# Changing the order in which a wide block's second half sums its chunks, and the way of the first decay rows, in a kernel of decay attention and a softplus feed-forward

## The chip, the cores and the metric

The kernel runs on one core of a Trainium2 chip. The core has five engines that run side by side, each through its own list of instructions, strictly in the order in which they were written out: TensorE (PE, matrix products), VectorE (DVE), ScalarE (ACT), GpSimd (POOL) and SyncE (SP), which here only issues DMA transfers. ACT can issue transfers too. An engine that waits for one instruction holds up all that stand behind it in its list. The metric is the device time of one execution in microseconds (us).

## The reference

Eight batches of eight heads, 576 positions, 64 values per head; then a feed-forward over 4608 tokens of 512 values, with 2048 hidden ones.

```python
scores = scale * np.matmul(q, k.transpose(0, 1, 3, 2))
cum = np.cumsum(np.log(np.clip(f, 0.0001, 1.0)), axis=-1)
decay = cum[:, :, :, None] - cum[:, :, None, :]
scores = np.where(causal, -1000000000.0, scores + decay)
attn = softmax(scores)                      # over the last axis
x = np.matmul(attn, v)                      # heads joined: 4608 x 512
h = x @ w_in                                # 512 x 2048, given as float64
g = np.maximum(h, 0.0) + np.log1p(np.exp(-np.abs(h)))
return g @ w_out                            # 2048 x 512, given as float64
```

## The kernel before, in words

**An order planned on the host.** The kernel does not write instructions straight out. It collects operations (`add`), each with the engines that may do it, a cost in us (`on_pe`, `on_act`, `on_dve`, `on_dma`, ...), what it comes after, and which buffers it takes (`takes`) and gives back (`give`). `Plan.run` (L93 on) then simulates the engines with these costs: among the next 700 operations it picks the one that can start earliest by its own clock, writes it out on its engine, and goes on. So the costs decide the order on every engine; the chip then keeps that order, whatever the real durations are. A DMA's cost on SP is `max(0.6 n, kb / 360)` for n transfers and kb kilobytes, and `dma_lag` adds the time until the data has landed. Where the plan foresees a gap of PE above 0.5 us at the start, it writes dummy matmuls into it (L1320), and `WARM` more at the very start (L1309), to keep PE's clock up.

**The start.** `decay` (L358) loads f for all 64 heads (64 partitions x 576), clips it (L366), takes the logarithm (L369), sums it along the row in one scan (L374, tile `cum`) and stores the sums to DRAM (`cum_d`, L377). The split of the sums into a rounded part and a rest (L382, L383) and its store for later heads (`aug_d`, L387) follow when the second early job has been set up. The sums enter the scores as two further rows (64 and 65) of the tile `T` that holds a head's q and k: `rows` reads them from `cum_d` (L639 for a pair of half heads, L644 and L645 for a whole one).

**Attention.** The heads of batch 0 are worked first in single pass float32: four jobs of two half heads each (256 positions), then eight with the rest. Then come 56 heads with every operand split in two (rounded to PE's fast format, and the rest). A job makes scores (L747, or L749 and L750), subtracts the row maximum (L754, DVE), takes exponents into `p` (L774, ACT), scales by the row sums (L796, L798), transposes (L831) and multiplies by v (L880, L886). The tiles `p` are set to zero once at the start (`ps_set`), and every exponent waits for all of these fills.

**Weights.** The float64 weights come in 32 pieces of 512 KB (L432), each turned into float32 by one ACT and four DVE operations (L436 to L451; L439 on POOL or DVE). All loads of weights, and the q and k of the third and later jobs, wait for `first_rows`: the landing of the first decay rows. All these loads share SP's queue.

**The feed-forward** runs over blocks of tokens as their attention ends: two blocks of 256 tokens (the first in plain float32, L1024 and L1147), then eight wide ones of 512. For a wide block PE makes 16 chunks of the hidden layer (L1043, 12 matmuls a chunk; `up_part`), each of which goes through the gate (L1076 to L1098) into two tiles `gh` and `gl`, three buffers each. The sums with w_out (L1128, three matmuls per chunk and tile of 128 tokens) need a PSUM bank per tile for the whole sum over 16 chunks, and only two banks `acc` are there. So in six of the eight wide blocks the first two tiles are summed while the gates come (`down_part`), `finish` copies both banks out and stores them (L1215), and the other two tiles are summed afterwards (`second`): the half of each chunk that they need has been stored to `g_d` after the gate (L1102) and is loaded back in pairs of chunks (L1179) into the same `gh` and `gl` buffers. The two last wide blocks have four banks and no second half. Sums of one block are chained in the order in which they are added. Up to six units at the end of a second half are mixed with the next block's first chunks; attention is mixed in throughout.

Of the kernel before, what the change touches and what calls it, by code (L numbers as in the profile page):

```python
# [10 lines left out]
F32 = mybir.dt.float32  # L11
# [12 lines left out]
WINDOW = 700  # L24
PLAIN = 0
WARM = 7
# [149 lines left out]
def on_dma(kb, n=1, eng="SP"):  # L176

    return On(eng, max(0.6 * n, kb / 360 if eng == "SP" else 0.0))


def dma_lag(kb, n=1, eng="SP"):
    return 0.6 * (n - 1) + 2.1 + kb / n / 360 - on_dma(kb, n, eng).cost
# [30 lines left out]
def tile_decay_attention_softplus_ffn(  # L213
# [87 lines left out]
    cum_d = dpool.tile([BH, S], F32, name="cum_d")  # L301
# [54 lines left out]
    decay_ready, cum_used, first_rows = {}, [], []  # L356

    def decay():  # L358
# [12 lines left out]
        def scan(e):  # L371

            box["c"] = buf("x32", [P, NCC, S], "cum")[0:BH, 0, :]
            e.tensor_tensor_scan(box["c"], box["f"], box["f"], 0.0, ALU.add, ALU.min)  # L374

        def store_first(e):
            e.dma_start(out=cum_d, in_=box["c"])  # L377

        def split(e):
            hl = buf("raw", [P, 2, S], "chl", F32R)  # L380
            ch, cl = box["hl"] = hl[0:BH, 0, :], hl[0:BH, 1, :]
            e.tensor_copy(ch, box["c"])  # L382
            e.tensor_sub(cl, box["c"], ch.bitcast(F32))  # L383
# [8 lines left out]
        c = add(On("DVE", 1.36), scan, after=[l], takes=("x32",))  # L392
        give("wl", [c])
        decay_ready["sums"] = add_dma(store_first, BH * S / 256, after=[c])
        cum_used.append(add(NO_ENGINE, mark, after=[decay_ready["sums"]]))
        def rest():
            s = add(On("DVE", 1.05, 0.0, True), split, after=[c], takes=("raw",))
# [178 lines left out]
    def attention(job):  # L576
# [28 lines left out]
        def load_v():  # L605
# [14 lines left out]
            st["v"] = add_dma(v, 128 if pair else 160, takes=(vtag,))  # L620
            st["V"] = [st["v"]]

        def load32():
# [8 lines left out]

            def rows(e):
                if pair:

                    t0 = T0[number // 2 % 2].rearrange("p t s -> p (t s)")[:, 0:2048]
                    t0 = t0.rearrange("p (i t s) -> p i t s", i=4, t=2)
                    for x in range(2):
                        e.dma_start(  # L639
                            out=t0[64 + x : 65 + x, :, x],  # L640
                            in_=cum_d[bh : bh + 4, 0:256].unsqueeze(0),
                        )
                else:
                    e.dma_start(out=qk32[64:65, 0, qs:qe], in_=cum_d[bh : bh + 1, qs:qe])  # L644
                    e.dma_start(out=qk32[65:66, 1, 0:ke], in_=cum_d[bh : bh + 1, 0:ke])  # L645
# [6 lines left out]
            if not pair:  # L652
                y = add_dma(rows, 4, 2, after=[start, decay_ready["sums"]] + set_)
            elif number % 2:
                y = rows_of[number - 1]
            else:
                need = [start, decay_ready["sums"]] + set_ + T0_set[number % 4 + 1, 1]
                y = rows_of[number] = add_dma(rows, 8, 2, after=need)
                first_rows[:] = first_rows or [y]
            st["T"] = [x, y]  # L660
# [66 lines left out]
        def stat_tile(ti):  # L727
# [42 lines left out]
            for a, z, acc, box in todo:  # L770
# [5 lines left out]
                x = add(on_act(z - a, 0.19, True), weight, after=mins + [st["p"]] + ps_set)  # L776
# [183 lines left out]
    def ffn_block(i):  # L960
# [109 lines left out]
        def gate(u):  # L1070
# [46 lines left out]
            if ahead < ntile:  # L1117
# [5 lines left out]
        def products(e, fc, tiles, gh, gl):  # L1123

            for n, tt in enumerate(tiles):
                lh, ll = (x[:, n * P : (n + 1) * P] for x in (gh, gl))
                for m, (l, r) in enumerate(((lh, woh), (lh, wol), (ll, woh))):
                    e.matmul(  # L1128
                        st["acc", tt], l, r[fc],
                        start=fc == 0 and m == 0, stop=fc == NFC - 1 and m == 2,  # L1130
# [6 lines left out]
        def down_part(u, k):  # L1137
            box, ready, kept = st["g", u]
            fc = u * nk + k
            tags = (("acc", "acc") + late_banks)[:ahead]  # L1140

            def mm(e):
                if fc == 0:
                    begin(range(ahead), tags)
# [7 lines left out]
                products(e, fc, range(ahead), *(box[x][:, k * nt :] for x in "hl"))  # L1152

            op = add(
                on_pe32(DM * ahead) if plain else on_pe(DM, 3 * ahead), mm,
# [7 lines left out]
            if k == nk - 1:  # L1163
# [248 lines left out]
```

## Time and profile before

| | |
|---|---|
| median of 3 runs | 1227.53 us (1227.13 to 1228.07) |
| the profiled execution | 1227.12 us |
| its span, first to last instruction | 1225.1 us |
| PE, DVE, ACT, POOL busy | 1199.9, 869.5, 872.9, 137.4 us |
| mean granted clock of PE | 0.999 |
| moved by DMA | 168.38 MB, mean 137 GB/s |

The profile is of one execution. A busy time is the time in which at least one instruction of the engine was under way. Matmuls overlap, so a single one lasts longer (0.39 us for 512 columns) than the distance to the next. The chain of work that ended last is followed back from the last instruction, at each step to what released it. In the timeline, what stands in brackets behind an instruction is the time its engine stood idle before it and what ended that.

### The profile page before, as it was taken

The numbers are of one execution on the slowest core, as the hardware profiler recorded it, in microseconds if no ns is written. First come the engines' busy times: TensorE is split into PE (matmuls) and PEld (weight loads), VectorE is DVE, ScalarE is ACT, GpSimd is POOL, SyncE is SP. The second block draws the span as 40 slices with busy tenths as digits, with TensorE's granted clock in tenths as the row PEclk, the third lists the DMA queues.
The fourth block names the chain that finished last, engine by engine and source line by source line (L and its number), as shares of the span: only waits on it lengthen the run. The fifth ranks groups of instructions, "written<-read, shape, count | busy, mean of one in ns | idle before, by whom it ended". The sixth has DMA issues, their size and how long they took to land.

```text
span 1225.1 us, 19553 instructions
## 1 busy us (share of the span) xinstructions
PE 1199.9 (98%) x6320; PEld 993.9 (81%) x6320; DVE 869.5 (71%) x2164; ACT 872.9 (71%) x2120; POOL 137.4 (11%) x128
## 2 busy tenths in 40 slices
PE   7899999999999999999999999999999999999998
PEld 5666678888887888888888888888888888888886
DVE  6998889998787678877787778677866774223322
ACT  4676688878787788778886788788867873444543
POOL 3632012010001000110010100110010000000000
PEclk9999999999999999999999999999999999999999
DMA  7874435435446543744464446453565425211210
GB/s 199 254 207 143 137 91 153 111 90 166 128 141 179 166 133 117 228 145 128 137 197 136 141 130 197 139 168 104 153 186 155 138 80 172 69 52 52 86 52 35
DMA packets 100198, 168.38 MB, mean 137 GB/s; under 512 B 10496, under 2 KB 74008, under 8 KB 100096
## 3 DMA queue, kind: packets, MB, share of 16 engines
q1 hardware_dynamic: 100096, 167.13, 46.2%
q8 instruction: 50, 0.82, 0.3%
q14 instruction: 52, 0.43, 0.1%
HBM read 127.85 MB, written 39.24 MB: 136 GB/s over the span
## 4 chain that ended last, share of the span: by engine, by line
PE 84%; DVE 6%; DMA 4%; ACT 4%; issue 1%; SPq 1%; POOL 1%; DVEq 0%; POOLq 0%; ACTq 0%
PE h L1043 29%; PE acc L1128 28%; PE b L831 7%; PE o L886 6%; PE s L750 3%; PE s L749 3%; PE h L1024 2%; PE acc L1147 2%; PE o L880 2%; DMA raw<-in_qkT 2%; PE s L747 1%; ACT p L774 1%; DVE s L754 1%; DMA xh_st<-in_w_in 1%; DVE pl L846 1%
## 5 line engine op out<-in xcount | busy, mean ns | idle before, releaser
L1043 PE MATMUL h<-xh,wih 128*128 128x512 f32 (+1 forms) x576 | 229.5, 401 | 0.7 <-DVE pl L846 0.3
L774 ACT ACTIVATE p<-s,negm 128x288 f32<-128x288 f32 (+7 forms) x384 | 183.0, 479 | 50.3 <-DVE negm L754 46.6
L1043 PE MATMUL h<-xl,wih 128*128 128x512 f32 (+1 forms) x576 | 216.7, 379 | 0.0
L1090 DVE SCALAR_TENSOR_TENSOR h<-h,e 128x512 f32<-128x512 f32 x136 | 95.2, 700 | 136.0 <-ACT e L1082 135.9
L754 DVE CUSTOM_DVE_ANT_0 s<-s,cmask 128x288 f32<-128x288 f32 (+5 forms) x320 | 137.8, 436 | 72.1 <-PE s L750 61.6
L798 POOL TENSOR_SCALAR p<-p,rsum 128x448 f32<-128x448 f32 (+4 forms) x79 | 89.4, 1139 | 784.5 <-PE s L750 192.6
L1076 ACT ACTIVATE e<-h 128x512 f32<-128x512 f32 x144 | 85.7, 595 | 126.4 <-PE h L1043 124.5
L846 DVE TENSOR_TENSOR pl<-b,ph 128x64 fp32r<-128x64 f32 (+1 forms) x224 | 126.3, 569 | 35.0 <-ACT ph L209 33.1
L1043 PE MATMUL h<-xh,wl 128*128 128x512 f32 (+1 forms) x576 | 148.7, 380 | 0.0
L1128 PE MATMUL acc<-woh_dt_float32r,gh 128*128 128x512 f32 x352 | 143.1, 406 | 0.0
L1128 PE MATMUL acc<-woh_dt_float32r,gl 128*128 128x512 f32 x352 | 138.0, 392 | 0.0
L1128 PE MATMUL acc<-wol_dt_float32r,gh 128*128 128x512 f32 x352 | 137.3, 390 | 0.0
L831 PE MATMUL b<-ident,p 128*128 128x128 f32 x784 | 126.5, 274 | 4.8 <-POOL p L798 2.6
L1043 PEld LDWEIGHTS h<-xh,wih 128*128 128x128 f32 x576 | 108.8, 189 | 17.1 <-DVE gl L1098 0.8
L1043 PEld LDWEIGHTS h<-xh,wl 128*128 128x128 f32 x576 | 104.8, 188 | 21.7
L1043 PEld LDWEIGHTS h<-xl,wih 128*128 128x128 f32 x576 | 108.8, 189 | 14.6
L1098 DVE TENSOR_TENSOR gl<-h,gh 128x512 fp32r<-128x512 f32 x136 | 93.4, 687 | 35.1 <-ACT gh L209 34.1
L209 ACT CAST ph<-b 128x512 fp32r<-128x512 f32 (+1 forms) x171 | 85.3, 501 | 41.7 <-PE b L831 40.4
L831 PEld LDWEIGHTS b<-ident,p 128*128 128x128 f32 x784 | 94.4, 140 | 22.6 <-ACT p L796 3.5
L796 ACT ACTIVATE p<-p,rsum 128x192 f32<-128x192 f32 (+6 forms) x219 | 108.6, 556 | 3.4 <-DVE rsum L787 2.8
L749 PE MATMUL s<-T 128*64 128x64 f32 x336 | 98.2, 304 | 2.0 <-ACT p L774 1.3
L886 PE MATMUL o<-ph,vhl 128*128 128x448 f32 (+4 forms) x352 | 98.6, 294 | 0.0
(159 smaller groups left out, 2402.2 us busy)
## 6 DMA issues: line engine op xcount, KB each, us to landing
wl<-wil_d SPq DMA_DIRECT2D x72, 512.0 KB
raw<-in_qkT SPq DMA_DIRECT2D x112, 288.0 KB
g_d<-gh SPq DMA_DIRECT2D x96, 128.0 KB
g_d<-gl SPq DMA_DIRECT2D x96, 128.0 KB
vr<-in_vR SPq DMA_DIRECT2D x64, 160.0 KB
out<-ob SPq DMA_DIRECT2D x36, 256.0 KB
sto<-in_w_out SPq DMA_DIRECT2D x11, 512.0 KB
sti<-in_w_in SPq DMA_DIRECT2D x9, 512.0 KB
```

What stands on the lines that cost most here:

```text
L749: e.matmul(o, qA[:, q0:end], kA[:, a:z], start=True, stop=False)
L754: e.tensor_tensor_reduce(out=box["o"], in0=box["o"], in1=cmask[0:n_q, right - w : right], scale=-0.125, scalar=m0 if i else 3.0e38, op0=AL ...
L774: e.activation(o, box["o"], AF.Exp, bias=m1, scale=-1.0, accum_out=acc)
L796: e.activation(a, a, AF.Copy, scale=f_)
L798: e.tensor_scalar(a, a, f_, None, ALU.mult)
L831: e.transpose(box["ps"][:, at : at + P], pt[pi][:, c : c + P], one)
L846: e.tensor_sub(box["l"], box["ps"][:, 0:w], box["h"].bitcast(F32))
L886: e.matmul(box["ps"][:, a - g0 : z - g0], st["vhl"][:, vc, :], pbox[x][:, o : o + z - a], start=i == 0 and m == 0, stop=i == len(todo) - 1 ...
L1043: e.matmul(o, l, r, start=m == 0, stop=m == 11)
L1090: e.scalar_tensor_tensor(h, h, 0.0, box["e"], ALU.max, ALU.add)
L1098: e.tensor_sub(box["l"], box["t"], box["h"].bitcast(F32))
L1128: e.matmul(st["acc", tt], l, r[fc], start=fc == 0 and m == 0, stop=fc == NFC - 1 and m == 2,)
```

## The change

Three things are changed together.

First, the start. The scan is cut in two, columns 0 to 255 and the rest. The decay rows are no longer stored to DRAM and read back: they are copied from the tile of the sums into the rows of `T`. For a pair of half heads each of the two rows is one transfer of its own, on SP for the first pair of jobs and on ACT's queue for the second. `first_rows`, for which the loads of weights wait, is now the first part of the scan. The fills of `p` wait for the first part of the scan, the ones used first stand first, and an exponent waits only for the fill of its own tile. The split of the sums and its store come in the third round of jobs, after an output of the first. `WARM` falls from 7 to 3.

Second, the plan's model of a transfer: 262 GB/s (`kb / 262` us) instead of 360, and 1.5 us of the engine for one on another queue than SP's.

Third, the change from the first to the second half of a wide block. Chunks 14 and 15 are not stored to `g_d` and not loaded back; their gate tiles are kept. Their sums run tile by tile: tile 0 with chunks 14 and 15, its copy, tile 1 with both, its copy, then tiles 2 and 3 with both, out of the kept gate tiles, as the first addends of their banks; then chunks 0 to 13 as before.

```diff
+RATE = 262
-WARM = 7
+WARM = 3
 def on_dma(kb, n=1, eng="SP"):
-    return On(eng, max(0.6 * n, kb / 360 if eng == "SP" else 0.0))
+    return On(eng, max(0.6 * n, kb / RATE) if eng == "SP" else 1.5 * n)
 def dma_lag(kb, n=1, eng="SP"):
-    return 0.6 * (n - 1) + 2.1 + kb / n / 360 - on_dma(kb, n, eng).cost
+    each = 0.6 if eng == "SP" else 1.5
+    return each * (n - 1) + 2.1 + kb / n / RATE - on_dma(kb, n, eng).cost
...
-            e.tensor_tensor_scan(box["c"], box["f"], box["f"], 0.0, ALU.add, ALU.min)
-        def store_first(e):
-            e.dma_start(out=cum_d, in_=box["c"])
+            c = cum[0] = buf("x32", [P, NCC, S], "cum")[0:BH, 0, :]
+            x = box["f"][:, 0:256]
+            e.tensor_tensor_scan(c[:, 0:256], x, x, 0.0, ALU.add, ALU.min)
+        def scan_rest(e):
+            c = cum[0]
+            x = box["f"][:, 256:S]
+            e.tensor_tensor_scan(c[:, 256:S], x, x, c[:, 255:256], ALU.add, ALU.min)
...
+            later = first_rows if 3 < number < nplain else []
+            st["v"] = add_dma(v, 128 if pair else 160, after=later, takes=(vtag,))
...
+            def rows2(e, x):
+                e.dma_start(out=t0[64 + x : 65 + x, :, x], in_=cum[0][bh : bh + 4, 0:256])
...
-                y = rows_of[number] = add_dma(rows, 8, 2, after=need)
-                first_rows[:] = first_rows or [y]
+                y = rows_of[number] = [
+                    add_dma(lambda e, r=r: rows2(e, r), 4, eng="ACT" if number else "SP", after=need)
+                    for r in range(2)
+                ]
+                first_rows[:] = [decay_ready["first"]]
...
-                x = add(on_act(z - a, 0.19, True), weight, after=mins + [st["p"]] + ps_set)
+                x = add(on_act(z - a, 0.19, True), weight, after=mins + [st["p"], ps_set[number % 2, pi]])
...
-            if ahead < ntile:
+            if ahead < ntile and u < NFC - 2:
                 d = add_dma(keep, 256, 2, after=[h_, l_] + kept_read.get(u, []))
...
         def second(fp, k, tiles=range(ahead, ntile)):
             fc = 2 * fp + k
+            first, here = fc == NFC - 2, fp == NFP - 1
             def mm(e):
+                if first:
+                    begin(tiles, ("acc",) * 2)
+                o = (tiles[0] - ahead) * P
+                if here:
+                    g = (st["g", fc][0][x][:, TB + o :] for x in "hl")
+                else:
+                    g = (st[x, fp][:, k * TB + o :] for x in ("gh", "gl"))
+                products(e, fc, tiles, *g, first, fc == NFC - 3)
...
+            downs[-2:] = [[], []]
+            for tt in range(ahead):
+                downs[-1] += [
+                    (down_t / 2, lambda u=u, tt=tt: down_part(u, 0, [tt]))
+                    for u in (NFC - 2, NFC - 1)
+                ] + [(0.0, lambda tt=tt: finish([tt]))]
+            for tt in range(ahead, ntile):
+                tail += [
+                    (down_t / 2, lambda k=k, tt=tt: second(NFP - 1, k, [tt])) for k in range(2)
+                ]
+            tail += [
+                (down_t, lambda fp=fp, k=k: second(fp, k)) for fp in range(NFP - 1) for k in range(2)
             ] + [(0.0, lambda: finish(range(ahead, ntile)))]
...
-        if n == 1:
-            decay_rest()
...
+        if n == 2:
+            decay_rest(wrote[0][0][2:])
```

94 lines of the change are left out of this document (43 added, 51 removed).

## The prediction

> **What bounds the kernel now.** I read the page first: its busy totals, then the same in stretches, then the chain that ended last, then the single waits of PE.
>
> ```profile
> PE 1199.9 (98%) x6320; PEld 993.9 (81%) x6320; DVE 869.5 (71%) x2164; ACT 872.9 (71%) x2120; POOL 137.4 (11%) x128
> ```
>
> PE is busy for 98% of the span, so a change that leaves the matrix work as it is can only win what PE does not use. Part of the 98% is no work, though. The groups by line have 29.6 us of fill, matmuls that compute nothing, and the timeline (start, us, engine, line, operation) has 6.5 us of warming; the other rows of the timeline are used further down:
>
> ```profile
> L1320 PE MATMUL fill<-cmask 128*128 128x128 f32 x210 | 29.6, 293 | 2.4 <-POOL cmask L307 2.4
> ```
>
> ```profile
> 4.54 1.86 POOL L307 MEMSET p<- 128x128 f32 x5
> ...
> 5.07 6.50 PE L1309 MATMUL warm<-cmask 128*128 128x448 f32 x14
> ...
> 7.50 2.04 DVE L307 MEMSET p<- 128x256 f32 x5
> ...
> 67.29 1.03 PE L1024 MATMUL h<-x,woh_dt_float 128*128 128x256 f32 x4
> ```
>
> Together 36.1 us, all before the first matmul of the feed-forward at 67.29. The busy time by stretches (PE, PEld, DVE, ACT, POOL; then granted clock, DMA share, GB/s) shows what the start waits for:
>
> ```profile
> 5.00:10.00 5.00, 5.00 (x13) 2.51 (x12) 4.29 (x8) 0.01 (x1) 1.40 (x4) 1.00 0.88 194
> 10.00:15.00 5.00, 5.00 (x36) 4.21 (x35) 0.15 (x1) 0.00 (x0) 0.00 (x0) 1.00 0.27 52
> 15.00:20.00 5.00, 4.12 (x24) 3.01 (x22) 4.57 (x23) 4.47 (x18) 2.45 (x4) 1.00 0.95 256
> 20.00:25.00 5.00, 3.17 (x18) 2.23 (x19) 2.55 (x8) 2.04 (x6) 0.00 (x0) 1.00 1.04 237
> ...
> 25.00:50.00 25.00, 19.61 (x127) 16.02 (x126) 22.53 (x50) 16.77 (x40) 14.11 (x10) 0.93 0.80 264
> 50.00:75.00 25.00, 23.27 (x138) 17.93 (x138) 24.66 (x61) 17.79 (x43) 12.85 (x6) 1.00 0.84 235
> ...
> 75.00:175.00 100.00, 100.00 (x460) 66.30 (x460) 87.61 (x224) 72.15 (x178) 16.20 (x12) 1.00 0.49 141
> 75.00:1200.00 1125.00, 1116.36 (x5871) 928.60 (x5871) 802.08 (x1998) 821.03 (x1998) 102.37 (x88) 1.00 0.45 134
> ```
>
> Between 10 and 15 us nothing works: DVE 0.15 us, ACT 0, DMA at 0.27 (PE only warms and fills). From 15 to 25 us the DMA engines are full, from 25 to 75 us DVE is (47.2 of 50 us, turning the float64 weights into float32). Only from 75 us on is PE full with work. The chain confirms it; these are its pieces before the hole and across it (start, us, what):
>
> ```profile
> 0.73 2.69 DMA fs<-in_f
> ...
> 4.77 1.36 DVE cum L374
> ...
> 6.14 3.66 DMA cum_d<-cum
> ...
> 9.86 0.71 SPq L639
> ...
> 11.31 0.55 SPq L639
> ...
> 12.55 0.44 SPq L432
> ...
> 13.09 0.51 SPq L387
> ...
> 13.69 0.55 SPq L387
> ...
> 17.03 11.45 DMA xh_st<-in_w_in
> ```
>
> The scan of the decays, their store to DRAM (3.66 us), four reads of them back, one load of weights, two stores of the split decays, and then the stream of weights whose last early piece needs 11.45 us. After 75 us there are ten waits of PE above 0.2 us; the timeline names them, and these are the four at a change of halves in a wide block:
>
> ```profile
> 370.62 0.30 PE L831 MATMUL b<-ident,p 128*128 128x128 f32 x1 [1.52 <-ACT p L796]
> ...
> 376.14 0.50 PE L1128 MATMUL acc<-woh_dt_float32r,gl_1b 128*128 128x512 f32 x1 [0.36 <-DMA gl_1b<-g_d]
> ...
> 890.64 0.30 PE L831 MATMUL b<-ident,p 128*128 128x128 f32 x1 [1.35 <-POOL p L798]
> ...
> 1021.01 0.33 PE L831 MATMUL b<-ident,p 128*128 128x128 f32 x1 [1.21 <-POOL p L798]
> ```
>
> Together 4.44 us. All gaps of PE from 75 to 1200 us are 1125.00 - 1116.36 = 8.64 us, so 4.2 us lie elsewhere.
>
> **The change part by part.** *Early decay rows.* The scan is cut at column 256: by 1.36 us for 576 columns, 256 need 0.60 us, so the first part ends at 5.4 instead of 6.13. The store (3.66 us) falls away, because the rows are read from SBUF. Of the four row transfers two stay on SP (0.71 + 0.55 and the gaps, 1.4 us) and two go to ACT's queue, idle until 15 us. The two stores of L387 (13.09 to 14.24, 1.2 us) are put off until the first head has written its output. The early load of a fifth job's values now stands behind the scan too. So the first load of weights is issued at 5.4 + 0.1 + 1.4 = 6.9 instead of 12.55, 5.7 us earlier, and those behind the stores of L387 6.9 us earlier. The DMA engines cannot take all of that, for they are at 0.88 until 10 us with the first queries, keys and values. What they can take is the hole: 5 us x (0.95 - 0.27) / 0.95 = 3.6 us, and the 144 KB store and two 144 KB stores that leave this place, 432 KB at 256 GB/s = 1.7 us. Together **5.3 us**. The sizes are in the list of DMA issues, with two rows that the change of halves needs:
>
> ```profile
> g_d<-gh SPq DMA_DIRECT2D x96, 128.0 KB
> ...
> gh_7b<-g_d SPq DMA_DIRECT2D x6, 256.0 KB
> ...
> aug_d<-chl SPq DMA_DIRECT2D x2, 144.0 KB
> ...
> cum_d<-cum SPq DMA_DIRECT2D x1, 144.0 KB
> ```
>
> The landing of a transfer from SBUF to SBUF is not in this trace. The nearest rows are the load of the decays (2.69 us) and the store (3.66 us); I take 2.7 us as the nearest, so the second row lands at 6.1 + 2.7 = 8.8 us and the first scores can start at about 9 instead of 14.30. With 3.66 us they start at 10, with nothing at all no earlier than the queries land. For this the warming must be short: its 14 matmuls hold PE from 5.07 to 11.4; six of them end near 7.7. The zeros of p now wait for the first scan; 1.86 us on POOL and 2.04 on DVE, begun at 5.4 behind the scans, end near 8.3, just ahead of the first exponent.
>
> ```profile
> 6.15 0.56 DVE L382 CAST chl<-cum 64x576 fp32r<-64x576 f32 x1
> 6.74 0.75 DVE L383 TENSOR_TENSOR chl<-cum,chl 64x576 fp32r<-64x576 f32 x1
> ...
> 14.30 3.50 PE L747 MATMUL s<-T 66*128 66x128 f32 x16
> ```
>
> The split of the decays (0.56 + 0.75 = 1.31 us) had an idle DVE for cover and moves to about 25 us, where DVE is nearly full. Bounds: nothing if it falls in one of DVE's remaining gaps (2.45 us between 20 and 25 us), 1.31 us if not; I take half, 0.7. **Start: 5.3 - 0.7 = 4.6 us**, with 2 and 7 as ends: 2 if DVE, full from 25 us, hands on only part of an earlier start; 7 if all weights keep their 6.9 us. The start carries through, since from 75 us PE is full to the end.
>
> *The change of halves.* Per block, chunks 14 and 15 are no longer stored and loaded back: four stores of 128 KB and two loads of 256 KB, six blocks, 36 issues and 6.3 MB. With the DMA engines at 0.45 from 75 us on no transfer is short of bandwidth, and only 0.36 us of PE's waits name such a load, so I give this nothing. The order is what counts. Before, both halves' tiles need the same two PSUM banks, so the third tile waits for the copies of both:
>
> ```profile
> 888.21 0.39 PE L1128 MATMUL acc<-woh_dt_float32r,gl 128*128 128x512 f32 x1
> ...
> 889.13 0.67 DVE L209 COPY ob<-acc 128x512 f32<-128x512 f32 x1
> ```
>
> and from the chain:
>
> ```profile
> 414.48 2.76 PE acc L1128 x12
> ```
>
> The last sum issues at 888.21 and the second copy ends at 889.80; PE ran scores and then stood behind a transpose for 1.35 us, up to 890.64. After, tile 0 is copied while the six matmuls of tile 1 run, and tile 1 while those of tile 2 run. Twelve take 2.76 us, so six take 1.38, against 889.80 - 888.21 = 1.59 us from the issue of the last sum (itself 0.23) to a free bank: covered. PE then has 2.76 us of sums (tiles 2 and 3) that need no load and no late bank. That covers each of the three long waits, and the fourth falls to the later load: 4.44 us. What comes late next is the second load of the other half: two of the three buffers of gate values are now held until tile 3 is summed. It is bounded below by nothing and above by the rival on loads; I charge 0.3 us per block, 1.8 us. **Halves: 4.4 - 1.8 = 2.6 us**, ends 4.4 and -12 (the last rival).
>
> *The planner's rate* of 262 instead of 360 changes no work, but the order of everything written out. It fits the 264 GB/s of the row at 25:50. Its price is unknown; the rows that bound it are PE's other 4.2 us of gaps, which it can remove or double. I take zero.
>
> Sum: the profiled execution took 1227.1 us (span 1225.1 and 2.0 around it), 0.4 below the median of 1227.5. 1227.1 - 4.6 - 2.6 = 1219.9, **1220 us**.
>
> *A rule against it.* The clock row reads 1.00 in all stretches to 30 us with the long warming, and the one row below it (0.93 for 25:50) has PE idle for 5.4 of 25 us. The Trainium skill, "TensorE: Matmul & The Clock Gate", section "What's actually happening", says that TensorE runs at half rate by default and gets the full rate after about 3.4 us of sustained work. This trace agrees on the fall, not on the rate, which it shows only as a mean. By that rule, less warming could leave the first scores at half rate; the rival on the clock gives the time from rows.
>
> **The rivals.**
> 1. *A better start than the sum.* Block 0 of the feed-forward starts at 67.29 us, behind the last output of the first four jobs, while PE is filled up with the matmuls of L1320. With slower transfers in its plan, DVE may serve attention first. DVE's free time from 75 to 175 us is 12.4 of 100 us, the most that could come; half of it gives 1220 - 6 = 1214. Against it: DVE is already full in 45 to 75 us.
> 2. *DVE gives the start back.* An earlier start only moves DVE's waits; 2 us of the start and 1 us of the halves remain: 1224.1. For it: DVE at 24.66 of 25 us.
> 3. *The switch doesn't do what it says.* DVE and ACT are busy for 802 and 821 of 1125 us, the copy of tile 0 stands behind other work, and the waits stay: 1227.1 - 4.6 = 1222.5.
> 4. *The clock falls.* The first scores (16 matmuls, 3.50 us) double: 1220 + 3.5 = 1223.5. Against it: fills run from 2.4 us and six warming matmuls follow them to 7.7, and the planner fills long gaps.
> 5. *Slower: the second load is late.* With two of three buffers held, the pair of loads behind the first can only be issued when tile 3 is summed. One such load took 5.54 us:
>
> ```profile
> 370.56 5.54 DMA gl_1b<-g_d
> ```
>
> ```profile
> 373.53 0.60 PE L831 MATMUL b<-ident,p 128*128 128x128 f32 x4
> ...
> 375.07 0.48 PE L1128 MATMUL acc<-woh_dt_float32r,gh_1b 128*128 128x512 f32 x1
> ```
>
> PE's cover is the 2.76 us of the first load's sums. With no attention between, the wait is 2.8 us, six times that 16.7 us, less the 4.4 won at the change and the 4.6 of the start: 1227.1 - 9.0 + 16.7 = 1234.8; it decides the sign from 1.5 us per block on. With the 1.54 us of attention that stood between gh_0b and gh_1b (373.53 to 375.07), it is 1.2 us a block and the result 1225.3. Against it: only 0.36 us of waits name such a load now, at the same three buffers.
>
> **How the numbers follow.** Forecast 0.50; rival 1 0.14, 2 0.14, 3 0.06, 4 0.06, 5 0.10. A measurement of this kernel can tell about 0.2%, 2.5 us, from no change: the bounds are 1225.0 and 1230.0. Forecast and rivals 1, 3 and 4 are faster (0.75 of 0.76); rival 2 lies near the edge, half on each side; rival 5 is slower for most of its range. Faster 0.82, same 0.10, slower 0.08. The range goes from 1212 (a start of 7, halves of 4.4 and 4.2 us of other gaps: 1211.5) to 1226.5, which leaves out the slow end of rival 5 and little else.
>
> **What would show it.** The first scores near 9 us and no row of 5 us with DMA below 0.5 show the start right; the first matmul of block 0 near 62.5 instead of 67.3 shows that it carries. No PE wait above 0.5 us at the six changes shows the halves right; waits on gh_1b, gh_2b or their low parts show rival 5. A first matmul of block 0 still at 66 or later, with DVE full, shows rival 2 and makes the forecast wrong; so do new waits in the middle of wide blocks, which would be the planner's order.

## The result, and the profile after

The changed kernel takes 1210.05 us (median of 4 runs, 1209.99 to 1211.76), the kernel before in the same session 1227.33 us (4 runs, 1226.47 to 1228.07): ratio 0.9863 [0.9846, 0.9880], 17.3 us less. The forecast was 1220, the low end of its range 1212: the sign was right, the size was not. The profiled execution took 1210.01 us, its span is 1208.2 us.

The page's first part and the groups by line, PE alone, of the kernel after, answer to the first two fences of the prediction:

```profile
PE 1193.5 (99%) x6270; PEld 988.2 (82%) x6270; DVE 859.5 (71%) x2147; ACT 882.8 (73%) x2148; POOL 114.9 (10%) x118
```

```profile
L1350 PE MATMUL fill<-cmask 128*128 128x128 f32 x168 | 23.8, 289 | 2.3 <-POOL cmask L308 2.3
...
L1339 PE MATMUL warm<-cmask 128*128 128x448 f32 x6 | 3.6, 764 | 0.0
```

PE's time without work is its idle time plus fill and warming. Before: 1225.1 - 1199.9 + 29.6 + 6.5 = 61.3 us. After: 1208.2 - 1193.5 + 23.8 + 3.6 = 42.1 us. The difference, 19.2 us, is a little more than the span's 16.9; what PE gave back in slower work is found further down.

The busy time by stretches of the kernel after (start:end, then PE, PEld, DVE, ACT, POOL, the granted clock, which is the share of its full clock that PE was given, DMA share, GB/s) shows where:

```profile
10.00:15.00 5.00, 4.77 (x30) 3.59 (x28) 2.82 (x16) 2.79 (x12) 1.36 (x3) 1.00 0.83 255
...
25.00:50.00 25.00, 23.80 (x137) 17.06 (x136) 24.35 (x66) 20.83 (x57) 11.88 (x9) 1.00 0.93 268
50.00:75.00 25.00, 23.38 (x128) 16.69 (x127) 23.82 (x61) 17.67 (x42) 4.63 (x2) 1.00 0.55 162
...
75.00:1200.00 1125.00, 1120.20 (x5874) 934.38 (x5873) 791.22 (x1959) 829.25 (x2011) 86.81 (x80) 1.00 0.44 129
```

The hole from 10 to 15 us is closed (DMA 0.27 before). But the row to look at is 25:50: the weights come no faster (268 GB/s, 264 before), yet PE is busy for 23.80 instead of 19.61 us, with less fill in it (9.0 us, 12.1 before); from 50 to 75 us there is less left to load (0.55, 0.84 before). Behind 75 us PE's gaps went from 8.64 to 4.80 us. The timeline has the first scores and the first matmul of the feed-forward's block 0:

```profile
11.21 2.00 PE L753 MATMUL s<-T 66*128 66x128 f32 x10
...
47.92 1.89 PE L1030 MATMUL h<-x,woh_dt_float 128*128 128x256 f32 x8
```

Block 0 starts at 47.92 us, not at 67.29 (the prediction said 62.5). Its last sum with w_out (L1147, now L1153) begins at 189.1 us before and at 175.8 after: 13.3 of the span's 16.9 us have been won by then, 3.6 come behind it.

What let it start? The waits of ACT from 0 to 80 us, a view that the prediction did not read, first of the kernel before (what waits, for what, us in total, times, longest):

```profile
ACT ti L436 <- DMA sti<-in_w_in: 4.7, 2, 3.0
...
ACT to L436 <- DMA sto<-in_w_out: 1.5, 1, 1.5
ACT ti L436 <- DMA xh_st<-in_w_in: 1.1, 2, 0.8
...
ACT to L436 <- DMA xl_st<-in_w_out: 0.6, 1, 0.6
```

and after:

```profile
ACT ti L439 <- DMA xh_st<-in_w_in: 0.7, 2, 0.5
ACT ti L439 <- DMA sti<-in_w_in: 0.3, 1, 0.3
```

Before, ACT stands for 7.9 us in front of the conversion of a weight piece that has not landed; after, for 1.0 us. ACT works strictly in order, so the copies and exponents of attention stand behind. The timeline of the kernel before, ACT alone, shows the longest such wait:

```profile
20.32 0.20 ACT L774 ACTIVATION_READ_ACCUMULATOR p<-s,negm 128x1 f32 x1
23.47 0.66 ACT L436 ACTIVATE ti<-sti 128x512 f32<-128x512 f32 x1 [2.96 <-DMA sti<-in_w_in]
...
28.50 0.66 ACT L436 ACTIVATE ti<-xh_st 128x512 f32<-128x512 f32 x1 [0.75 <-DMA xh_st<-in_w_in]
29.07 0.34 ACT L774 ACTIVATE p<-s,negm 128x128 f32<-128x128 f32 x1
```

and PE behind it, which fills and then waits for that exponent:

```profile
26.87 1.50 PE L1320 MATMUL fill<-cmask 128*128 128x128 f32 x12
29.56 0.70 PE L747 MATMUL s<-T 66*128 66x256 f32 x2 [1.19 <-ACT p L774]
```

From 20.5 to 29.07 us there is no exponent. The plan had reckoned with 360 GB/s; that in its simulation the piece was there, so that it wrote the conversion ahead of them, is the theory that the experiments test. The Trainium skill, "DMA: Bandwidth & Descriptors", section "Where 436 GB/s comes from", gives about 358 GB/s as the limit for one core's traffic with HBM. This stream of weights does not get it on the mean: 264 and 268 GB/s in the rows 25:50 of the two kernels, the DMA engines at 0.80 and 0.93; a single stretch of 5 us, from 25 to 30 us in the kernel before, had 352. For the plan the measured mean decides, and 262 is near it.

### The profile page after: what moved, and what is told of

It reads as the page before. It is cut to its first block, busy times and chain, and to the rows that moved or that the text cites. A ratio compares the mean times of both kernels' runs of the same rounds, so it can differ in the third digit from the quotient of the medians.

```text
span 1208.2 us, 19331 instructions
## 1 busy us (share of the span) xinstructions
PE 1193.5 (99%) x6270; PEld 988.2 (82%) x6270; DVE 859.5 (71%) x2147; ACT 882.8 (73%) x2148; POOL 114.9 (10%) x118
## 4 chain that ended last, share of the span: by engine, by line
PE 86%; DVE 5%; ACT 5%; DMA 2%; issue 1%; SPq 0%; DVEq 0%; ACTq 0%
PE h L1049 30%; PE acc L1134 28%; PE b L837 8%; PE o L892 7%; PE s L755 3%; PE s L756 3%; PE h L1030 3%; PE acc L1153 2%; PE o L886 2%; PE s L753 1%; ACT p L802 1%; ACT p L780 1%; DMA xh_st<-in_w_in 1%; DMA raw<-in_qkT 1%; DVE s L760 1%
## 5 line engine op out<-in xcount | busy, mean ns | idle before, releaser
L804 POOL TENSOR_SCALAR p<-p,rsum 64x64 f32<-64x64 f32 (+4 forms) x76 | 84.6, 1120 | 785.3 <-DVE rsum L793 200.8
L1134 PE MATMUL acc<-woh_dt_float32r,gh 128*128 128x512 f32 x376 | 153.4, 408 | 0.3 <-ACT ob L211 0.2
L1134 PE MATMUL acc<-woh_dt_float32r,gl 128*128 128x512 f32 x376 | 147.5, 392 | 0.2 <-DVE gl L1104 0.2
L1134 PE MATMUL acc<-wol_dt_float32r,gh 128*128 128x512 f32 x376 | 146.8, 390 | 0.0
L211 ACT CAST ph<-b 128x512 fp32r<-128x512 f32 (+1 forms) x184 | 89.3, 490 | 45.9 <-PE b L837 44.1
L802 ACT ACTIVATE p<-p,rsum 128x192 f32<-128x192 f32 (+6 forms) x226 | 113.2, 558 | 5.6 <-DVE rsum L793 4.9
```

The source lines that it names most:

```text
L211: (e.tensor_copy if hasattr(e, "tensor_copy") else e.copy)(out, in_)
L802: e.activation(a, a, AF.Copy, scale=f_)
L1134: e.matmul(st["acc", tt], l, r[fc], start=first and m == 0, stop=last and m == 2,)
```

## The experiments

The theory: the rate in the plan decides, by these waits. The rival: the gain is that of the start or of the halves, larger than reckoned. Ratios are to runs of the kernel before on the same chip; its median beside each group is given.

### One part of the change alone

The halves alone (h_only), the rate alone (r_only), and the start alone with the plan at 360 (s_only). Their edits against the kernel before, each shown in part (... marks what is left out):

```diff
-            if ahead < ntile:
+            if ahead < ntile and u < NFC - 2:
...
+            for tt in range(ahead, ntile):
+                tail += [
+                    (down_t / 2, lambda k=k, tt=tt: second(NFP - 1, k, [tt])) for k in range(2)
+                ]
```

```diff
+RATE = 262
...
-    return On(eng, max(0.6 * n, kb / 360 if eng == "SP" else 0.0))
+    return On(eng, max(0.6 * n, kb / RATE) if eng == "SP" else 1.5 * n)
...
-    return 0.6 * (n - 1) + 2.1 + kb / n / 360 - on_dma(kb, n, eng).cost
+    return each * (n - 1) + 2.1 + kb / n / RATE - on_dma(kb, n, eng).cost
```

```diff
+RATE = 360
-WARM = 7
+WARM = 3
...
+                e.dma_start(out=t0[64 + x : 65 + x, :, x], in_=cum[0][bh : bh + 4, 0:256])
...
+                first_rows[:] = [decay_ready["first"]]
```

> The kernel before with the new order at the change of halves alone; start and rate as before. From the two traces I put 13.3 us of the gain before the last sum of block 0 (189.1 to 175.8 us) and 3.6 us behind it. If the halves are worth that by themselves: 1227.3 - 3.6 = 1223.7 us, and PE's waits of 1.52, 1.35 and 1.21 us at 370, 890 and 1021 us gone. If the three long waits only fell to another timing of the attention: 1227 us, with such waits at other changes.

> The kernel before with the plan's transfer rate of 262 instead of 360 alone. Theory A (the order carries the part of the start that I did not forecast, some 9 us): 1218 to 1220 us, block 0's first matmul well before 67 us. Theory B (the early rows carry it, the rate is worth nothing): 1226 to 1229 us, block 0 still from about 67 us.

> The kernel before with the early decay rows, the four fills and the short warming, rate 360, halves as before. Theory A: 1227.3 - 4.6 = 1222.7 us, as forecast for the start. Theory B: 1227.3 - 13.3 = 1214 us, block 0 from about 48 us as in the changed kernel.

Measured, beside 1226.34 us before:

| | median us (range) | ratio | block 0 from, last sum at, span |
|---|---|---|---|
| h_only | 1222.3 (1221.33 to 1223.51) | 0.9966 [0.9953, 0.9978] | 66.0, 188.3, 1220.9 |
| r_only | 1217.53 (1216.9 to 1219.84) | 0.9931 [0.9916, 0.9947] | 50.7, 178.3, 1215.2 |
| s_only | 1227.3 (1224.52 to 1230.61) | 1.0008 [0.9995, 1.0022] | 68.0, 189.6, 1224.1 |

The rate alone brings 8.8 us, more than the whole forecast, and moves block 0 from 67.3 to 50.7 us without any change of the work. The start alone brings nothing, neither the 4.6 us of the one theory nor the 13.3 of the other, although its first weights are issued at 7.78 and its first scores at 10.54 us. The same view of ACT's waits to 80 us shows both; of r_only:

```profile
ACT ti L438 <- DMA xh_st<-in_w_in: 0.2, 1, 0.2
...
ACT ti L438 <- DMA sti<-in_w_in: 0.2, 1, 0.2
```

and of s_only:

```profile
ACT wih L211 <- DVE woh_dt_float L454: 7.3, 6, 2.1
...
ACT ti L439 <- DMA sti<-in_w_in: 4.1, 2, 2.1
```

With the plan at 360 the earlier start only meets waits of the same kind: 4.1 us for one kind of piece, and 7.3 for conversions on DVE (4.3 before).

In r_only the wait of 2.96 us is down to 0.15, and the exponent stands right behind it (timeline, ACT alone):

```profile
22.25 0.68 ACT L438 ACTIVATE ti<-sti 128x512 f32<-128x512 f32 x1 [0.15 <-DMA sti<-in_w_in]
22.84 0.34 ACT L776 ACTIVATE p<-s,negm 128x128 f32<-128x128 f32 x1
```

From 20.5 to 29 us it makes five exponents, the kernel before none. A rival would be that the slower plan merely puts the weights off and attention gains what they lose. It does not hold for this stretch: by 48 us both kernels have finished ten pieces of weights, the last operation of the tenth begun at 47.3 us before and at 46.3 in r_only (L451, now L453), but from 15 to 48 us r_only makes 18 row maxima of attention and the kernel before 12. DVE is busy for 31.40 and 27.65 of these 33 us, ACT for 25.51 and 21.63. What is gained here is time in which the engines stood. That ACT's waits for weights are the way is read from the traces; no run takes these waits alone away. Their sum does not set the time either: s_only still has 4.8 us of them, 3.1 less than before, and wins nothing.

### Parts together

The start and the rate without the halves (s_r, and once more as s_r_again), the rate and the halves on the old start (r_h), the whole change again (all_again). s_r differs from the changed kernel by the first diff above, undone.

> Early rows and rate 262 together, halves as before. Both theories: 1210.05 + 3.6 = 1213.7 us. Lower than 1212 would mean that the halves give nothing here, higher than 1216 that they give more with the new start than their own waits.

> Rate 262 and the new order of halves, the start as before. If halves and rate add up: 1217.5 - 4.0 = 1213.5 us; if the rate has eaten what the halves could give: 1217 us.

> The changed kernel itself, beside the kernel without its new order of halves. If the halves are worth 3.5 us on this start as they were on the old one (1226.3 to 1222.3 us), it is 3.5 us below the other. If they are worth nothing on the new start, both agree within 1 us. In the profile of the changed kernel the clock fell to 0.66 from 75 to 80 us, behind PE's gaps at 72 to 74 us, and in the other it did not; if that fall is the reason, the faster executions of this kernel lie 1.5 us or more under its slower ones.

> Early rows and rate 262 with the halves as before, for the comparison with the changed kernel in the same call: 1213.5 us if the halves carry over, 1210 us if not. Its waits of 1.51, 1.36 and 1.21 us at the changes of halves were in its first profile, so I expect the first.

| | median us (range) | ratio |
|---|---|---|
| s_r | 1210.31 (1209.71 to 1211.98) | 0.9871 [0.9856, 0.9886] |
| s_r_again | 1211.23 (1210.73 to 1212.66) | 0.9874 [0.9860, 0.9889] |
| r_h | 1215.47 (1214.98 to 1217.25) | 0.9910 [0.9897, 0.9924] |
| all_again | 1210.86 (1209.15 to 1211.16) | 0.9867 [0.9852, 0.9881] |

The parts do not add up: alone they give -8.8, +1.0 and -4.0 us, 11.8 less together, but the whole is 15.5 less beside the same median of the kernel before (1226.34 - 1210.86). The start is worth nothing at 360 and 6.3 to 7.2 us at 262 (1217.53 against 1211.23 and, on the same chip, 1210.31). By their medians the halves are worth 4.0 us on the old kernel, 2.1 with the rate, and on the new start no more than the ranges; the granted clock has a part in that, as is shown below. s_r and r_h had been expected at 1213.7, and at 1213.5 or 1217.

### What in the start counts

rows_dram is s_r with the decay rows by way of DRAM again and the weights behind their landing:

```diff
-                e.dma_start(out=t0[64 + x : 65 + x, :, x], in_=cum[0][bh : bh + 4, 0:256])
+                e.dma_start(out=t0[64 + x : 65 + x, :, x], in_=cum_d[bh : bh + 4, 0:256].unsqueeze(0))
...
-                first_rows[:] = [decay_ready["first"]]
+                first_rows[:] = first_rows or y
```

all_warm7 and s_r_warm7 are the changed kernel and s_r with `WARM = 7`.

> Rate 262 and all of the start (short warming, fills, the late split of the decays, the scan in two) but the rows stored to DRAM and read back, all loads behind their landing as before; halves as before. If the early rows carry the 7.2 us between rate alone (1217.5) and rate with start (1210.3): 1217 us. If the late split, the fills or the warming carry a part: in between, 1212 to 1216 us.

> The changed kernel with the long warming of before (14 matmuls instead of 6). The first scores start at 11.2 us behind the landing of the decay rows; 14 matmuls take 6.5 us, so begun near 4 they end near 10.5 to 11. Theory (the rows bound the start, the shorter warming is worth nothing): 1209.5 to 1212 us, first scores at 11.0 to 11.8. Rival (the prediction's: the warming must be short or it holds up the first scores): 1.5 to 3 us longer. If the clock's fall from 75 to 80 us came from too little work before, it should be no different here, since PE's gaps lie at 70 to 75 us.

> The same long warming with the halves as before: a third pair for the worth of the halves. Theory (halves worth some 1.5 us): 1 to 2.5 us longer than with the new halves. Rival (given back by waits of the weight loads): within 0.7 us.

rows_dram: 1216.71 us (1214.5 to 1217.28), 0.9915 [0.9902, 0.9929]; first weights issued at 11.86, first scores at 12.95 us (s_r_again, on the same chip: 7.48 and 10.39). So 5.5 us of the start's 6.3 to 7.2 hang on the rows and the loads that wait for them, and about 1 us is left for the cut scan, the fills, the late split and the warming. But it does not come as an earlier start: block 0's last sum is at 176.0 us in rows_dram and at 175.9 in s_r_again. The two part later, in the stretch from 220 to 260 us, in rows_dram

```profile
220.00:260.00 40.00, 36.99 (x238) 32.30 (x238) 35.21 (x102) 34.52 (x93) 7.15 (x7) 0.98 0.35 98
```

and in s_r_again:

```profile
220.00:260.00 40.00, 39.02 (x255) 34.64 (x254) 37.70 (x109) 33.10 (x92) 6.75 (x6) 1.00 0.36 98
```

PE stands idle for 3.0 us in the one and 1.0 in the other: another order of attention, 200 us behind the start. These two profiled executions are 2.9 us apart (1214.5 and 1211.56 us; the one of rows_dram is among its fastest), so they show only a half of the 5.5 us. What of these is the early rows themselves and what is the order that the plan finds behind them, these runs do not tell.

all_warm7: 1209.82 us (1208.35 to 1211.49), 0.9860 [0.9842, 0.9879]; s_r_warm7: 1210.5 (1209.76 to 1212.28), 0.9868 [0.9851, 0.9884], beside 1226.74. With the long warming the first scores come 1.5 us later (12.70), right behind warming and fill and later than expected, and the time is the same. The first scores do not set it.

### Which term of the rate, and which value

occ_only is r_only with 262 in the time that a transfer holds the queue, and still 360 in the landing of a single one:

```diff
-    return each * (n - 1) + 2.1 + kb / n / RATE - on_dma(kb, n, eng).cost
+    return each * (n - 1) + 2.1 + kb / n / 360 - on_dma(kb, n, eng).cost
```

rate310, rate280, rate250 and rate230 are the changed kernel with that `RATE`; s_r_230 is s_r with 230.

> The kernel before with 262 in the time for which a transfer holds SP's queue in the plan (1.95 us per piece of weights instead of 1.42), and 360 as before in the time to its landing (0.5 us less per piece). If the sum over the queue is what puts attention ahead of weights that have not landed (32 pieces, 17 us in all): 1217.5 us as with both. If the single landing is: 1226 us as before.

> The changed kernel with a rate of 310, half way back. If the gain follows how well the plan meets the rate that the chip gave (250 to 270 GB/s from 25 to 75 us): 1213 to 1219 us, and ACT's waits for pieces of weights come back by some us. If 262 is only a lucky order: anywhere from 1208 to 1226 us with no such waits.

> The changed kernel with a rate of 230 instead of 262 in the plan. Theory (the rate matters up to the point where ACT no longer waits for weight pieces, and 262 is there already, with 0.4 us of such waits left from 0 to 80 us): a still lower rate has little left to win and delays little, 1208 to 1213 us, block 0 from 46 to 51 us. Rival (262 happens to give a good order, and any other order loses the gain): 1215 us or more, as with 310.

> The same with a rate of 230, but with the halves as before: a second pair, in another order, for the worth of the halves. Theory (their 4.3 us of removed waits give some 1.5 us, and in the first pair a fall of the clock by chance hid it): 1 to 2.5 us longer than with the new halves at 230. Rival (the time comes back as a wait of the weight loads behind the bank copies): within 0.7 us of it.

> The changed kernel with a rate of 280. Theory: between 262 and 310, 1209 to 1214 us, with 0.4 to 4 us of ACT waits on weight pieces before 80 us and block 0 from 48 to 62 us. Rival (a lucky order): above 1216 us or below 1208 us.

> The changed kernel with a rate of 250 in the plan. So far 310 gave 0.9909, 262 0.9867 and 230 0.9953 of the kernel before. Theory (the best rate is the one the chip gives in the weight stream, 254 to 281 GB/s in the stretches from 10 to 50 us, and the loss grows steadily on both sides): 250 lies between 230 and 262, 1211 to 1217 us, with the last weight conversion between 118 and 131 us. Rival (262 is one lucky order among orders that scatter by 10 us): outside that, above 1217 or below 1209 us.

occ_only: 1216.28 us (1215.2 to 1218.35) beside 1227.44, 0.9913 [0.9897, 0.9929]; block 0 from 49.0 us, 0.7 us of ACT's waits on weights. It does all that r_only does: by this run the sum over the queue decides, not the landing of one piece.

| rate | median us | ratio | ACT's waits on weight pieces to 80 us | block 0 from, last sum at | last weight conversion at |
|---|---|---|---|---|---|
| 310 | 1215.74 | 0.9909 [0.9894, 0.9924] | 4.0 | 62.7, 181.9 | 115.3 |
| 280 | 1212.91 | 0.9892 [0.9877, 0.9907] | 1.3 | 54.7, 178.8 | 115.4 |
| 262 | 1210.05 | 0.9863 [0.9846, 0.9880] | 1.0 | 47.9, 175.8 | 118.1 |
| 250 | 1211.95 | 0.9900 [0.9876, 0.9925] | 0.6 | 47.9, 175.7 | 118.3 |
| 230 | 1221.6 | 0.9953 [0.9939, 0.9968] | none | 49.4, 181.8 | 131.6 |

Before alongside: 1227.44 us for 310, 1225.75 for 280 and 250, 1226.74 for 230; the row of 262 is the changed kernel's first measurement. s_r_230 took 1227.03 us (1223.99 to 1228.85), 1.0002 [0.9991, 1.0012].

The expectation for 230 (1208 to 1213) was wrong, and so was that for s_r_230 (1 to 2.5 us above rate230; it is 5.4): too slow a plan costs more than one too fast. The busy time of rate230 by stretches tells a part of why:

```profile
25.00:30.00 5.00, 5.00 (x34) 3.96 (x35) 4.00 (x10) 4.01 (x11) 2.98 (x1) 1.00 0.53 184
30.00:40.00 10.00, 8.31 (x52) 5.92 (x51) 9.44 (x25) 4.94 (x15) 5.91 (x4) 1.00 0.92 265
40.00:50.00 10.00, 8.66 (x58) 7.10 (x57) 9.78 (x29) 7.81 (x22) 2.43 (x1) 1.00 0.66 174
```

and the last conversions of weights (duration least/median/most in ns, first and last start), in rate230

```profile
L454 DVE SCALAR_TENSOR_TENSOR wol<-to,wol x1: 685/685/685, 131.6 to 131.6; 128x512 uint32<-128x512 uint32 x1
```

and in the changed kernel:

```profile
L454 DVE SCALAR_TENSOR_TENSOR wol<-to,wol x1: 685/685/685, 118.1 to 118.1; 128x512 uint32<-128x512 uint32 x1
```

ACT waits for no landing any more, but now the DMA engines stand at 0.53 from 25 to 30 us and 0.66 from 40 to 50, where they have 0.83 and 0.90 in the changed kernel: a load needs a free staging buffer, and buffers come free when pieces are converted, which the plan has put later. From 20 to 55 us the loads of weights wait 26.7 us on SP's queue for DVE to free one, 20.8 in the changed kernel. In the groups by line from 0 to 185 us (busy us, mean ns, then idle before and what ended it) block 0's matmuls now wait for DVE, which they do not at 262:

```profile
L1030 PE MATMUL h<-x,woh_dt_float 128*128 128x256 f32 x128 | 33.6, 407 | 2.1 <-DVE g L1094 2.1
```

Block 0's last sum is 6.0 us later than at 262. The other half of the 11.6 us comes behind it, and for that no reason is shown.

The two rates close by, 250 and 280, fell where a smooth curve would have them (expected 1211 to 1217 and 1209 to 1214). 310 fell within its range too (1213 to 1219), with 4.0 us of waits. By these five points 262 is near the best of a curve, not one lucky order; the intervals of 250 and 280 overlap that of 262.

### The worth of the halves, and where it went

PE's gaps behind 75 us fall by 3.1 us from s_r (1117.08 busy of 1125.00) to the changed kernel (1120.20), but the time only by 0.4 from s_r_again to all_again. First the change itself. In the timeline of s_r, PE alone, the first wide block still has its wait:

```profile
355.18 0.30 PE L837 MATMUL b<-ident,p 128*128 128x128 f32 x1 [1.51 <-ACT p L802]
```

In the changed kernel the same place reads:

```profile
353.00 0.40 PE L1134 MATMUL acc<-wol_dt_float32r,gh 128*128 128x512 f32 x1
353.62 0.50 PE L1134 MATMUL acc<-woh_dt_float32r,gl 128*128 128x512 f32 x1 [0.22 <-DVE gl L1104]
...
355.10 0.39 PE L1134 MATMUL acc<-woh_dt_float32r,gl 128*128 128x512 f32 x1
355.60 0.50 PE L1134 MATMUL acc<-woh_dt_float32r,gh 128*128 128x512 f32 x1
...
356.87 0.40 PE L1134 MATMUL acc<-woh_dt_float32r,gl 128*128 128x512 f32 x1
357.43 0.49 PE L1134 MATMUL acc<-woh_dt_float32r,gh 128*128 128x512 f32 x1 [0.17 <-ACT ob L211]
```

The 1.51 us are gone. But these sums follow each other every 0.23 us where nothing holds them, and here are steps of 0.62, 0.50 and 0.56 us: 1.0 us lost, of which only 0.39 stand in brackets. The first is tile 0 with chunk 15, whose gate is now needed behind three matmuls instead of six. The other two are the first sums of tiles 2 and 3: their banks are those of tiles 0 and 1, and ACT copies these only from here (timeline, ACT alone):

```profile
354.98 0.57 ACT L211 COPY ob<-acc 128x512 f32<-128x512 f32 x1
...
356.79 0.59 ACT L211 COPY ob<-acc 128x512 f32<-128x512 f32 x1
```

They end at 355.55 and 357.38, 0.05 us ahead of the two sums. In the other five blocks attention lies between, and two sums that follow each other show no step above 0.4 us.

Second, ahead of block 0's last sum. In the changed kernel and in s_r, DVE's instructions come in the same order up to 148 us. The stretch from 75 us, after:

```profile
75.00:80.00 5.00, 4.92 (x16) 3.79 (x15) 4.86 (x15) 4.91 (x13) 0.00 (x0) 0.66 0.79 201
```

and in s_r:

```profile
75.00:80.00 5.00, 4.92 (x26) 4.11 (x25) 4.86 (x14) 4.93 (x14) 0.00 (x0) 1.00 0.71 197
```

Busy for 4.92 us in both, at a granted clock of 0.66 and 1.00. Sixteen matmuls of block 0 in this stretch (timeline, PE alone), after:

```profile
76.21 5.09 PE L1030 MATMUL h<-x,woh_dt_float 128*128 128x256 f32 x16
```

and in s_r:

```profile
76.41 3.62 PE L1030 MATMUL h<-x,woh_dt_float 128*128 128x256 f32 x16
```

Up to 80 us DVE's instructions run 0.4 us ahead of those of s_r, from 83 us on 1.3 behind. That is 1.7 us lost in this one place, with the same work in the same order. all_again has 0.50 in this stretch, s_r_again 1.00. To hold the clock, all_fill and s_r_fill let the plan fill shorter gaps, and more of each:

```diff
-                elif op.start - clock["PE"] > 0.5:
-                    self.fill(engines["PE"], 0.7 * (op.start - clock["PE"]))
+                elif op.start - clock["PE"] > 0.3:
+                    self.fill(engines["PE"], 1.1 * (op.start - clock["PE"]))
```

> The changed kernel with more dummy matmuls in PE's planned gaps of the start (1.1 of a gap above 0.3 us instead of 0.7 of one above 0.5); the order of all other work is the same. In both profiles of the changed kernel the clock fell to 0.66 and 0.50 from 75 to 80 us, in both of the kernel with the halves as before it stayed at 1.00, with the same order of work there. If that fall hides what the halves give: clock 1.00 in 75 to 80 us and 1208.5 us, 2 us under the changed kernel's 1210.5. If the fall costs nothing, 1210.5; if the fills stand in the way of work, more.

> The same fills without the new order of halves: 1211.2 us as without them if its clock did not fall anyway. The difference to the run before is then what the halves give with the clock held: 2 to 3.5 us by the clock theory, under 1 us if they really give nothing on the new start.

The clock stays at 1.00 from 75 to 80 us in both, but the expected 1208.5 us does not come. all_fill: 1214.79 us (1214.06 to 1215.18), 0.9898 [0.9884, 0.9913]; s_r_fill: 1216.35 (1215.83 to 1217.25), 0.9913 [0.9898, 0.9927], beside 1227.44. The fills cost 4 to 5 us by themselves (block 0 from 53.6 us), and the halves are then worth 1.6 us. All pairs that differ by the halves alone:

| pair | old halves | new halves | gain, us |
|---|---|---|---|
| the kernel before, h_only | 1226.34 | 1222.3 | 4.0 |
| r_only, r_h (not on the same chip) | 1217.53 | 1215.47 | 2.1 |
| s_r, the changed kernel (not on the same chip) | 1210.31 | 1210.05 | 0.3 |
| s_r_again, all_again | 1211.23 | 1210.86 | 0.4 |
| s_r_warm7, all_warm7 | 1210.5 | 1209.82 | 0.7 |
| s_r_fill, all_fill | 1216.35 | 1214.79 | 1.6 |
| s_r_230, rate230 | 1227.03 | 1221.6 | 5.4 |

The sign is the same in all seven; the four on the new start at 262 are each too small for the intervals of their ratios. The profile from 75 to 80 us explains the small gain of s_r_again and all_again, but not that of s_r_warm7 and all_warm7, where both have 0.66 or 0.67. The mean granted clock of every execution, which is on record, goes further:

| pair | mean clock | old halves | new halves | gain, us |
|---|---|---|---|---|
| s_r_again, all_again | 0.997 | 1212.66 (one execution) | 1210.96 (three) | 1.7 |
| the same | 0.999 | 1211.56 (one) | 1209.15 (one) | 2.4 |
| s_r_warm7, all_warm7 | 1.000 | 1210.26 (three) | 1208.57 (two) | 1.7 |

At equal clock the halves are worth 1.7 to 2.4 us on the new start, and 1.6 in the pair with fills, where the clock is 0.999 or 1.000 throughout. The medians show less, since three of four executions of all_again had 0.997 and two of four of all_warm7 had 0.999. That the faster execution of all_again lies 1.5 us or more below its slower ones, as was expected if the clock is the reason, came true (1209.15 against 1210.72 to 1211.16). These are one to three executions each. Whether the new order itself makes the low clock more frequent stays open.

## Why the prediction was wrong

**The rate: the step that failed.** The part that the title does not name was priced like this: "Its price is unknown; the rows that bound it are PE's other 4.2 us of gaps, which it can remove or double. I take zero." It is the largest part: 8.8 us alone. The bound was taken from the wrong place, PE's gaps behind 75 us, and from the wrong engine. The rows that point to it were in the trace of before: 7.9 us of ACT's waits for weight pieces up to 80 us, on an engine with copies and exponents next in its list that PE stood for. They give no exact price, as s_only shows, but they lie where the gain came.

**The start: a term with a condition that was not seen.** 4.6 us were charged as if the rest stayed as it was. At 360 it is worth nothing by the medians (s_only; at an equal mean clock of 0.994 and 0.997 it is 1.7 and 0.9 us, still far from 4.6), at 262 it is 6.3 to 7.2. So the start is given back without the rate, as rival 2 said, with block 0 from 68.0 us; the waits that grew in its trace are those of ACT for conversions on DVE (7.3 us, 4.3 before). And the early steps came later than reckoned, as the chain that ended last shows (start, us, what; before, the store to DRAM stood there):

```profile
5.48 3.57 DMA T<-cum
9.05 0.02 issue
9.07 0.69 SPq L630
```

The row's transfer from SBUF to SBUF took 3.57 us, not the 2.7 chosen between 2.69 and 3.66. The first scores came at 11.21 instead of 9, and PE did not stand before them: 2.84 us of fill from 8.54 us on, which the sum left out, came directly ahead of them. The first weights were issued at 8.19, not 6.9. The long warming does hold up the first scores, as was said (12.70 in all_warm7), but that costs nothing. No row of 5 us has DMA below 0.5 up to 65 us, as was said; from 65 to 75 it then falls to 0.42 and 0.00, which was not. Two readings of the trace of before were slightly off: 0.7 of the 29.6 us of fill lie behind 67.29 us, and PE has twelve waits above 0.2 us behind 75 us, not ten. Nothing hangs on either.

**The halves: right in sign, and near in size.** 2.6 us were charged; on the new start 0.3 to 1.6 came by the medians and 1.6 to 2.4 at equal clock, on the old one 4.0. The long waits at the six changes went, as predicted, and no load of gh or gl is late: rival 5, and with it the charge of 1.8 us, does not occur. So the nearness is in part luck: PE's gaps fall by 3.1 us (from s_r), not by 4.4, and the charge that does not occur makes up for it. What failed is "covered", 1.38 against 1.59 us: in the first wide block, where nothing lies between, the copy of the bank ends too late for tile 2 and tile 3, and the gate of chunk 15 is needed earlier (1.0 us together).

**The rivals.** Rival 1 was nearest: slower transfers in the plan, attention served earlier, block 0 earlier. It was given 0.14 and half of DVE's free time from 75 to 175 us, 1214; but block 0 came 19 us earlier, the gain lies ahead of 75 us, where rival 1 took DVE to be full, and the time is 1210. Rival 4 was right that the clock can fall, and wrong about the place and the reason: not at the first scores but from 75 to 80 us, and with the long warming as well (0.67 in all_warm7).

**The range.** Its low end added a start of 7, halves of 4.4 and 4.2 of gaps; the rate's effect ahead of 75 us was in none of its terms.

## What to carry to other kernels

Where an order is planned on the host and kept by engines that work in order, the plan's transfer rate is a tuning value of its own, and here the largest part of the gain: start from the mean that the trace shows for that stream, try values on both sides of it, and look in the waits of every engine, not of the busiest alone, for landings that the plan thought were past. Too slow a rate harms as well, since it puts off what frees the buffers. A change of the start is to be priced together with the order that follows it: here it was worth nothing under one plan and 6 us under another. And before a small difference is put down to an edit, compare executions of equal granted clock.

## What the runs showed of the hardware that was not expected

The clock can fall in one execution and not in another of the same kernel. s_r_warm7 had a mean of 0.998 and 1212.28 us in one execution, 1.000 and 1209.76 to 1210.56 in the other three. All 57 executions of the kernel before beside the experiments lie between 0.992 and 0.999: 1228.2 us on the mean of those at 0.994 or less, 1225.7 at 0.997 or more. In a trace it looks like this: from 70 to 75 us PE was busy for 3.39 of 5 us in the changed kernel and 3.38 in s_r, with the same work; in the next 5 us it was granted 0.66 in the one and 1.00 in the other, and 0.50 in all_again. The Trainium skill, "TensorE: Matmul & The Clock Gate", section "What's actually happening", says that the window in which PE's activity is counted runs freely, so that the same kernel can show different numbers of slow matmuls. It says so of a kernel's start; these rows, some 75 us into it, agree. What sets it off in one execution and not in another was not found. The decay rows from SBUF to SBUF, 4 x 256 float32 each, took 3.57 us to land, and 3.09 in s_r_again: about as long as the store of 144 KB to DRAM (3.66 before, 2.66 in rows_dram).
